# Weighted values as float32 products with two heads side by side, in a fused attention and SoLU kernel on one core

## The chip, the core and the metric

The kernel runs on one NeuronCore of a Trainium2 chip. Its engines each have their own instruction queue and run it in order: TensorE (PE in the profile, with its weight loads listed apart as PEld), VectorE (DVE), ScalarE (ACT), GpSimd (POOL) and SyncE (SP), which here only issues DMAs. The metric is the device time of one execution in microseconds; lower is better.

## What is computed

Attention with 4 sink keys and a causal window of 128 keys, and then a SoLU feed-forward layer on its output. Everything is float32.

```python
batch, n_heads, seq, head_dim = (4, 8, 768, 64);  n_sink, window = (4, 128)
scores = scale * np.matmul(q, k.transpose(0, 1, 3, 2))
keep = is_sink | in_window                    # rel = query - key, 0 <= rel < window
scores = np.where(keep, scores, -1000000000.0)
a = softmax(scores)
attn_out = np.matmul(a, v)
x = attn_out.transpose(0, 2, 1, 3).reshape(B * S, H * D)      # 3072 tokens, 512 wide
h = x @ w_in                                  # 512 -> 1024
sm = softmax(h); solu = h * sm
ln = (solu - mu) / np.sqrt(var + 1e-06) * g_ln
out = ln @ w_out                              # 1024 -> 512
```

q, k and v have the shape (4, 8, 768, 64). The weights arrive as 64-bit floats and are turned into 32-bit ones by integer work on the chip.

## The kernel before, in words

The 3072 tokens are worked in 24 chunks of 128. A chunk n is one block of 128 positions of one batch; `place(n)` (L472) gives its batch and its position c from 0 to 5, and two batches alternate, so that the chunk before in the same batch is n - 2. For c > 0 a chunk sees the keys of its own block, of the block before and of the sinks; for c = 0 (chunks 0, 1, 12 and 13) its own block alone.

TensorE multiplies in a rounded format (fp32r) at full rate, or in float32, which takes more passes. To keep float32 accuracy in fp32r most operands are split in a rounded first part and a rest, and two or three products are added. Chunks 0 and 1 are "native" (`native`, L551): they use plain float32 products for scores and values instead.

A chunk goes through these steps:

- `load_q`, `load_k`, `load_v`: DMAs on SP's queue. `turn_q`, `turn_k` (L533) transpose on TensorE; `take_*` (ACT) and `rest_*` (DVE) make the two parts; `swap_q` exchanges the halves by DMA.
- `score` (L604): two fp32r matmuls a head; `pick` and `mask` (DVE) choose the columns, add the mask and find the maximum; `exps` (ACT), `invert` (DVE), `normalise` (POOL).
- `turn_p` (L658) transposes the probabilities, four heads at a time; `p_hi` (ACT, L664) and `p_lo` (DVE, L668) split them; `part_new` and `part_old` (POOL, L675 and L682) cut out the part that belongs to the chunk's own block and that of the block before.
- `v_hi` (ACT, L502) and `v_lo` (POOL, L507) split v. `sink_values` (L513), once a batch, splits the first keys' values and spreads them over the pairs of heads; `sinks_hi`, `sinks_lo`, `turn_sinks`, `take_sinks` (L708, two ACT operations) do it for the sinks' probabilities.
- `value` (L715), one step for each of the four pairs of heads: for c > 0 five fp32r matmuls 256 wide into an accumulator of its own, in which first and second parts lie side by side. `gather` (DVE, L738) adds them, `shift` (L747) moves the halves that are on the wrong partitions by two DMAs, `tokens` (POOL, L755) adds these, and `x_hi` (ACT, L764) and `x_lo` (POOL, L768) split the result, half a chunk at a time. In the native chunks `value` writes two heads to the two halves of the partitions (L724), and there is no gather, shift or tokens.
- `hidden` (L775): eight steps of three fp32r matmuls, 512 wide. `highest`, `peak` (DVE), `solu_exp` (ACT), `solu` (DVE), `centre`, `square` (ACT), `variance` (DVE), `root` (POOL) make the SoLU and the normalisation. `turn_u`, `u_hi`, `u_lo`, then `project` (L846): eight steps of three fp32r matmuls; `scale` (ACT) and `store` (DMA).

The weights come in 16 blocks of 128 x 512: blocks 0 to 7 are w_in, 8 to 15 w_out. Each goes through `fetch_w` (DMA), `lower_w` (ACT, L419), `move_w`, `sign_w`, `rest_w` (DVE), `w_hi` (ACT, L453: the rounded part, for w_out times the gain). The second part is made with TensorE: `sum_w` (L446) multiplies the block in float32 by a negative diagonal from `gains` (L439), `less_w` (L463) adds the rounded part, and `w_lo` (ACT, L467) takes the negative of it:

```python
nc.tensor.matmul(t, st["dg", KT2 if j < NW1 else j - NW1], st["w", j], start=True, stop=False)
nc.tensor.matmul(st["ws", j], ident_r, part(wh, kt, cols), start=False, stop=True)
nc.scalar.mul(part(wl, kt, cols), st["ws", j], -1.0)
```

`idle` (L268) issues 33 float32 matmuls of the identity with itself, whose result nobody reads.

The order in which instructions enter the queues is written out by hand: every step has a time in `PLAN`, `FIRST`, `OWN` or `PLAN_W`, and the steps are issued in the order of these times (L876 to L881). The times only order the steps; the waits between engines are by semaphores. PSUM holds two buffers of one bank each for accumulators (`ps_acc`: values, sinks' transposes, project), two for scores and q and k transposes, two for the transposes of p and u, and two banks for h.

## Time and profile before

| | |
|---|---|
| three timed runs | 495.76, 496.22, 497.36 us (median 496.22) |
| the profiled execution | span 495.5 us from its first to its last instruction; its own time is not given apart from that |
| TensorE busy | 474.3 us (96%) |
| VectorE busy | 390.5 us (79%) |
| ScalarE busy | 354.2 us (71%) |
| GpSimd busy | 317.5 us (64%) |
| moved by DMA | 51.80 MB, mean 105 GB/s |
| granted TensorE clock, mean | 0.990 |

Matmuls are pipelined: the profile gives each one's start and a modelled end, so neighbours overlap. What one costs on TensorE's queue is the step from its start to the next one's. A float32 matmul that is not a transpose is two records. A group's row reads: line, engine, operation, output and inputs by the program's names, partitions x elements, count; then the busy time in us and the mean ns of one; then the idle time of the engine just before it and what ended most of it.

### The profile page before, as it was taken

Reading aid. Unit: us, or ns where it says so; the run is one execution under the profiler, and the core shown is the slowest. Engines: PE = TensorE matmul, PEld = TensorE weight load, DVE = VectorE, ACT = ScalarE, POOL = GpSimd, SP = SyncE. Lnnn points to the kernel's source line nnn. Section 1 sums busy time; section 2 is a strip of 40 time slices with the busy share of each in tenths; the row PEclk is TensorE's granted clock in tenths of the full one; section 3 lists DMA queues with packets and bytes.
Section 4 is the critical chain, followed back from the end, with each engine's and each line's share of the span. In section 5 each row is a group of like instructions: output and inputs, shape, how many; then the busy total and the mean of one; then the engine's idle time right before and its main releaser. Section 6 shows DMA issues by size and latency. Waiting matters only on the chain.

```text
span 495.5 us, 9225 instructions
## 1 busy us (share of the span) xinstructions
PE 474.3 (96%) x2697; PEld 395.1 (80%) x2697; DVE 390.5 (79%) x1195; ACT 354.2 (71%) x957; POOL 317.5 (64%) x439
## 2 busy tenths in 40 slices
PE   5988999999899999999999999999999999999994
PEld 5455767888788888888888888888888888888873
DVE  2888999899987588797799988888889879765631
ACT  3799997778776567776876787677777787675352
POOL 3677477587766557678646487576776776667610
PEclk9799999999999999999999999999999999999998
DMA  8976254354256363423365263364264262201101
GB/s 281 302 198 170 65 108 111 71 140 95 60 133 124 69 128 79 115 67 80 94 147 115 59 145 76 101 140 105 54 142 105 59 141 58 59 27 44 43 23 48
DMA packets 101100, 51.80 MB, mean 105 GB/s; under 512 B 78956, under 2 KB 90228, under 8 KB 101044
## 3 DMA queue, kind: packets, MB, share of 16 engines
q1 hardware_dynamic: 101044, 51.14, 42.6%
q8 instruction: 24, 0.39, 0.4%
q14 instruction: 32, 0.26, 0.2%
HBM read 27.53 MB, written 6.42 MB: 69 GB/s over the span
## 4 chain that ended last, share of the span: by engine, by line
PE 69%; DVE 15%; ACT 7%; issue 4%; POOL 3%; DMA 1%; SPq 0%; DVEq 0%; POOLq 0%
PE o L851 21%; PE h L782 20%; PE s L616 4%; PE utp L836 3%; PE av L731 3%; PE s L617 3%; PE av L734 3%; PE ptp L662 3%; DVE y L744 2%; DVE ring L589 2%; PE qt L536 2%; PE ws L451 2%; DVE sc L634 2%; PE kt L536 2%; PE av L736 2%
## 5 line engine op out<-in xcount | busy, mean ns | idle before, releaser
L851 PE MATMUL o<-w2h,uh 128*128 128x512 f32 x192 | 79.2, 413 | 0.0
L782 PE MATMUL h<-w1h,xh 128*128 128x512 f32 x192 | 77.5, 404 | 0.6 <-DVE u L804 0.6
L644 ACT ACTIVATE sc<-sc,nmx 128x136 f32<-128x136 f32 (+1 forms) x192 | 76.4, 402 | 1.7 <-DVE nmx L634 1.3
L782 PE MATMUL h<-w1l,xh 128*128 128x512 f32 x192 | 75.8, 395 | 0.0
L851 PE MATMUL o<-w2h,ul 128*128 128x512 f32 x192 | 75.7, 394 | 0.0
L782 PE MATMUL h<-w1h,xl 128*128 128x512 f32 x192 | 75.7, 394 | 0.0
L851 PE MATMUL o<-w2l,uh 128*128 128x512 f32 x192 | 75.7, 394 | 0.0
L744 DVE TENSOR_REDUCE y<-av 128x256 f32<-128x512 f32 x88 | 60.3, 686 | 19.5 <-PE av L736 18.8
L679 POOL TENSOR_SCALAR_AFFINE_SELECT pc<-pt 128x1024 fp32r<-128x1024 f32 x40 | 43.9, 1097 | 33.0 <-DVE pt L672 16.8
L655 POOL TENSOR_TENSOR sc<-sc,rs 128x544 f32<-128x544 f32 (+1 forms) x48 | 52.6, 1097 | 15.0 <-DVE rs L650 7.7
L634 DVE CUSTOM_DVE_ANT_0 sc<-s,bias 128x136 f32<-128x136 f32 (+1 forms) x192 | 54.3, 295 | 8.4 <-PE s L614 2.1
L616 PE MATMUL s<-ring,qT 128*128 128x264 f32 (+1 forms) x176 | 56.2, 321 | 2.8 <-DVE nmx L634 1.8
L771 POOL TENSOR_TENSOR xl<-xt,xh 128x256 fp32r<-128x256 f32 x44 | 32.5, 740 | 28.6 <-ACT xh L766 22.3
L617 PE MATMUL s<-ring,qX 128*128 128x264 f32 (+1 forms) x176 | 49.6, 284 | 0.3 <-DMA qX<-qT 0.3
L731 PE MATMUL av<-pc,vs 128*128 128x256 f32 x160 | 44.2, 299 | 1.3 <-ACT ob L856 0.9
L685 POOL TENSOR_SCALAR_AFFINE_SELECT pt<-pt 128x1024 fp32r<-128x1024 f32 x40 | 43.8, 1094 | 1.6
L782 PEld LDWEIGHTS h<-w1h,xl 128*128 128x128 f32 x192 | 36.1, 188 | 8.9 <-POOL xl L771 0.2
L840 ACT CAST uh<-utp 128x512 fp32r<-128x512 f32 x48 | 28.0, 586 | 21.2 <-PE utp L836 20.9
L844 DVE TENSOR_TENSOR ul<-utp,uh 128x512 fp32r<-128x512 f32 x48 | 33.0, 687 | 12.9 <-ACT uh L840 12.2
L851 PEld LDWEIGHTS o<-w2h,ul 128*128 128x128 f32 x192 | 36.1, 188 | 8.7 <-DVE ul L844 0.2
L616 PEld LDWEIGHTS s<-ring,qT 128*128 128x128 f32 x176 | 33.2, 188 | 12.0 <-issue 3.5
L584 ACT CAST ring<-kt 64x512 fp32r<-64x512 f32 x44 | 25.4, 578 | 22.9 <-DVE ring L589 21.8
(149 smaller groups left out, 1315.5 us busy)
## 6 DMA issues: line engine op xcount, KB each, us to landing
qX<-qT SPq DMA_DIRECT2D x88, 128.0 KB, 2.3
kn<-in_k_dram SPq DMA_DIRECT2D x24, 256.0 KB, 3.7
qn<-in_q_dram SPq DMA_DIRECT2D x24, 256.0 KB, 4.0
vn<-in_v_dram SPq DMA_DIRECT2D x24, 256.0 KB, 4.3
out_dram<-ob SPq DMA_DIRECT2D x24, 256.0 KB, 3.2
ysh<-y SPq DMA_DIRECT2D x88, 64.0 KB, 2.0
wraw<-in_moe_w_out_dram SPq DMA_DIRECT2D x8, 512.0 KB, 3.8
wraw<-in_moe_w_in_dram SPq DMA_DIRECT2D x8, 512.0 KB, 6.5
```

Of the source, the lines that this page charges most:

```text
L616: nc.tensor.matmul(o, st["qT", n, x][:, r, :], rhs, start=True, stop=False)
L617: nc.tensor.matmul(o, st["qX", n, x][:, r, :], rhs, start=False, stop=True)
L634: nc.vector.tensor_tensor_reduce(out=st["sc", n, hb][:, j, c0:c1], in0=st["s", n, h].rearrange("p a x -> p (a x)")[:, c0:c1], in1=bias0 if ...
L644: nc.scalar.activation(sc[:, i, c0:c1], sc[:, i, c0:c1], AF.Exp, bias=nmx[:, i:i + 1], scale=-1.0, accum_out=ssum[:, i:i + 1])
L655: nc.gpsimd.tensor_tensor(sc[:, :, c0:c1], sc[:, :, c0:c1], rs.unsqueeze(2).to_broadcast([P, HB, c1 - c0]), op=ALU.mult)
L679: nc.gpsimd.affine_select(pc, pt.bitcast(F32), pattern=[[0, HB * 2], [1, P]], compare_op=ALU.is_ge, fill=0.0, base=0, channel_multiplier=-1)
L685: nc.gpsimd.affine_select(pt, pt.bitcast(F32), pattern=[[0, HB * 2], [-1, P]], compare_op=ALU.is_ge, fill=0.0, base=-1, channel_multiplier=1)
L731: nc.tensor.matmul(acc[:, x], lhs, pc[:, 2 * jp + x], start=(x == 0), stop=(alone and x == 1))
L744: nc.vector.tensor_reduce(st["y", n, hb][:, jp], st["acc", n, pr].rearrange("p x s q -> p x q s"), axis=AX.X, op=ALU.add)
L782: nc.tensor.matmul(st["h", n][:, cols], a[:, kt % 2, :], w[:, kt, cols], start=(kt == 0 and m == 0), stop=(kt == KT1 - 1 and m == 2))
L844: nc.vector.tensor_tensor(ul, st["utp", n, g4], st["uh", n, g4].bitcast(F32), op=ALU.subtract)
L851: nc.tensor.matmul(st["o", n], a[:, kt % 4, :], part(w, kt), start=(kt == 0 and m == 0), stop=(kt == KT2 - 1 and m == 2))
```

## The change

- `value` becomes one step a chunk: for every pair of heads it multiplies plain float32 v by plain float32 probabilities, one head into the lower and one into the upper half of the partitions, for the chunk's own block and (c > 0) the block before, all into one accumulator of 512 columns. The native chunks use the same step.
- The sinks come first: `value_sinks` adds two fp32r matmuls, 512 wide. Their weights are a block-diagonal tile of the sink values (`sink_values`), and `take_sinks` spreads the probabilities over the four pairs by one DVE product.
- `v_hi`, `v_lo`, `p_lo`, `gather`, `shift` and `tokens` are gone, `p_hi` is called `take_p`, and the two selects work on half as many elements. `x_hi` (ACT) and `x_lo` (now DVE) read the accumulator once a chunk.
- The second part of a w_out block is one DVE operation (block times gain, less the rounded part) in place of `sum_w`, `less_w` and the ACT operation. w_in's blocks stay as they were. `idle` is gone.
- v has five buffers in place of two, p four of half the size in place of three.
- All the plans are replaced by one list, `ORDER`, with every step's place. In it w_in's block 6 is the first block to be fetched, lowered and moved; in the plan before, `fetch_w` began with block 10, `move_w` with block 6. 2614 steps stand in place of 3103.

```diff
-    def idle(_, j):
-        if "idle" not in st:
-            st["idle"] = ps_acc.tile([P, P], F32, tag="acc", name="idle")
-        nc.tensor.matmul(st["idle"], ident, ident, start=True, stop=True)
...
-    def gains(_, kt):
-        dg = st["dg", kt] = sb.tile([P, P], F32, tag="xt", name=f"dg_{kt}", bufs=2)
...
+    def gains(_, j):
+        st["minus"] = sb.tile([P, P], F32, tag="xl", name="minus", bufs=2)
+        nc.scalar.mul(st["minus"], ident, -1.0)
...
     def w_lo(_, j):
-        _, wl, _, kt, cols = blocks[j]
-        nc.scalar.mul(part(wl, kt, cols), st["ws", j], -1.0)
+        wh, wl, _, kt, cols = blocks[j]
+        if j < NW1:
+            nc.scalar.mul(part(wl, kt, cols), st["ws", j], -1.0)
+        else:
+            nc.vector.scalar_tensor_tensor(part(wl, kt, cols), st["w", j], g_sb[:, kt:kt + 1],
+                                           part(wh, kt, cols).bitcast(F32), op0=ALU.mult, op1=ALU.subtract)
...
+            vk = st["vsink", b] = sb.tile([P, 2, P], F32R, tag="vsink", name=f"vsink_{b}", bufs=2)
+            for x, m in enumerate((even, odd)):
+                cols = slice(x * D, (x + 1) * D)
+                nc.scalar.activation(vk[:, 0, cols], raw, AF.Copy, scale=m)
+                nc.vector.scalar_tensor_tensor(vk[:, 1, cols], raw, m, vk[:, 0, cols].bitcast(F32),
+                                               op0=ALU.mult, op1=ALU.subtract)
...
+    def take_p(n, hb):
+        pt = st["pt", n, hb] = sb.tile([P, HB, P], F32, tag="pt", name=f"pt_{n}_{hb}", bufs=4)
+        nc.scalar.copy(pt, st["ptp", n, hb])
...
-            for i, m in enumerate((even, odd)):
-                nc.scalar.activation(skt[:, i, :], tr.bitcast(F32), AF.Copy, scale=m)
+            skt = st["skt", n] = sb.tile([P, NPAIR, P], F32R, tag="skt", name=f"skt_{n}", bufs=2)
+            nc.vector.tensor_tensor(skt, st["skp", n].bitcast(F32).unsqueeze(1).to_broadcast([P, NPAIR, P]),
+                                    mine.to_broadcast([P, NPAIR, P]), op=ALU.mult)
+    def accumulator(n):
+        if ("acc", n) not in st:
+            st["acc", n] = ps_acc.tile([P, NPAIR, P], F32, tag="acc", name=f"av_{n}")
+        return st["acc", n]
+    def value_sinks(n, _):
         b, c = place(n)
+        if c > 0:
+            for t in range(2):
+                nc.tensor.matmul(accumulator(n), st["vsink", b][:, t, :], st["skt", n], start=(t == 0), stop=False)
+    def value(n, _):
+        alone = place(n)[1] == 0
+        acc = accumulator(n)
+        for r in range(NPAIR):
+            hb, jp = divmod(r, HB // 2)
+            terms = [(n, st["pt" if alone else "pc", n, hb])] + ([] if alone else [(n - 2, st["pt", n, hb])])
+            for i, (m, p) in enumerate(terms):
+                for x in range(2):
+                    nc.tensor.matmul(acc[ROWS[x], r, :], st["vn", m][:, 2 * r + x, :], p[:, 2 * jp + x, :],
+                                     start=alone, stop=alone or (r, i) == (NPAIR - 1, 1))
+    def x_hi(n, _):
+        xh = st["xh", n] = sb.tile([P, NPAIR, P], F32R, tag="xh", name=f"xh_{n}", bufs=2)
+        nc.scalar.copy(xh, st["acc", n])
+    def x_lo(n, _):
+        xl = st["xl", n] = sb.tile([P, NPAIR, P], F32R, tag="xl", name=f"xl_{n}", bufs=2)
+        nc.vector.tensor_tensor(xl, st["acc", n], st["xh", n].bitcast(F32), op=ALU.subtract)
...
-    for at, _, n, i, f in sorted(steps, key=lambda s: s[:4]):
+    for at in ORDER:
+        f, n, i = steps[at]
         f(n, i)
```

More of the change, by code (lines that the diff above doesn't have):

```diff
@@ L495, in load_v @@
     def load_v(n, _):
[L496 removed]
+        load(n, "vn", v, 5)
         b, c = place(n)
@@ new lines, in _banded @@
+    start = {
+        fetch_small: 3, round_ident: 1, gains: 1, scalars: 1, spread: 2, take_small: 2, masks: 3, outside: 1,
+        fetch_w: len(blocks), lower_w: len(blocks), move_w: len(blocks), sign_w: len(blocks), rest_w: len(blocks),
+        sum_w: NW1, w_hi: len(blocks), less_w: NW1, w_lo: len(blocks),
+    }
+    steps = [(f, 0, j) for f, k in start.items() for j in range(k) if k < NW1]
+    steps += [(f, 0, j) for j in range(len(blocks)) for f, k in start.items() if k >= NW1 and j < k]
@@ L881, in _banded @@
+    steps += [(f, n, i) for n in range(NCH) for f, k in stages.items() for i in range(k)]
+    for at in ORDER:
+        f, n, i = steps[at]
         f(n, i)
```

225 lines of the change are left out of this document (17 added, 208 removed), and 185 rows, old and new, of tables (ORDER, OWN).

## The prediction

> **What bounds the kernel now.** I read the page first, then the busy time by stretches (rows: stretch, its length, then busy time and instructions of PE, PEld, DVE, ACT, POOL; then the granted TensorE clock, DMA share, GB/s), then the chain of waits at the end, and last TensorE's instructions one by one where the trace holds the operations that the change adds.
>
> ```profile
> span 495.5 us, 9225 instructions
> PE 474.3 (96%) x2697; PEld 395.1 (80%) x2697; DVE 390.5 (79%) x1195; ACT 354.2 (71%) x957; POOL 317.5 (64%) x439
> ```
>
> ```profile
> 0.00:12.00 12.00, 6.91 (x46) 6.82 (x46) 2.38 (x6) 4.24 (x8) 3.43 (x18) 0.99 0.84 281
> 12.00:25.00 13.00, 11.63 (x39) 6.22 (x39) 11.25 (x30) 9.98 (x25) 8.54 (x13) 0.75 1.02 301
> 25.00:70.00 45.00, 40.79 (x216) 27.10 (x215) 39.95 (x124) 43.16 (x113) 30.16 (x47) 1.00 0.58 141
> 70.00:475.00 405.00, 401.24 (x2339) 344.43 (x2338) 331.47 (x1025) 290.46 (x805) 274.31 (x361) 1.00 0.40 93
> 475.00:496.00 21.00, 13.74 (x65) 10.58 (x63) 5.48 (x14) 6.32 (x10) 1.10 (x2) 0.93 0.08 29
> ```
>
> ```profile
> 473.93 2.11 PE h L782 x9
> ...
> 484.98 4.16 issue
> 489.13 0.69 ACT ob L856
> ```
>
> There are three regimes. From 70 to 475 us PE is busy for 401.24 of 405 us: here only what is on PE's own queue counts, and 3.8 us of gaps are all that better cover could win. Up to 70 us no engine is alone: ACT works 43.16 of the 45 us after 25, PE 40.79, DVE 39.95; ACT is the fullest. The tail (last project matmul, scale, store) has the same steps before and after, and I leave it alone. The profiled span is 495.5 us; the three timed runs are 495.76, 496.22 and 497.36, so I make the sum on the span and add 0.7 for the median. About 0.3% (1.5 us) is what a measurement here can tell from no change.
>
> **The change part by part: w_out's second parts leave PE.** Columns of the timeline: start, time, engine and line; what PE pays is the step from one start to the next, since the ends overlap.
>
> ```profile
> 72.47 1.02 PE L451 MATMUL ws<-wbits,dg 128*128 128x512 f32 x2
> 72.92 0.68 PE L731 MATMUL av<-pc,vs 128*128 128x256 f32 x1
> 73.44 0.28 PE L734 MATMUL av<-pt,vs 128*128 128x256 f32 x1
> 73.56 0.28 PE L731 MATMUL av<-pc,vs 128*128 128x256 f32 x1
> 73.67 0.28 PE L734 MATMUL av<-pt,vs 128*128 128x256 f32 x1
> 73.80 0.28 PE L736 MATMUL av<-skt,vsink 128*128 128x256 f32 x1
> 73.92 0.39 PE L465 MATMUL ws<-w2h,ident_r 128*128 128x512 f32 x1
> 74.14 0.60 PE L536 MATMUL qt<-ident,qn 128*128 128x128 f32 x4
> ```
>
> The float32 sum starts at 72.47 and the matmul after the next starts at 73.44; with 0.12 for the one between, the sum holds PE for 0.85 us. The subtraction on L465 takes 0.22 (73.92 to 74.14). Eight blocks: 8 x 1.07 = 8.6 us off PE. PE's records of this tile behind 70 us (three a block, float32 being two):
>
> ```profile
> 70.00:100.00 30.00, 2.88 (x6) 1.04 (x6) 1.17 (x2) 1.00 0.37 87
> ```
>
> So two blocks fall behind 70 us and six, 6.4 us, into the start-up.
>
> **The weighted values.** Before, a chunk behind the first of its batch issues 4 pairs x 5 fp32r matmuls at 0.118 (the steps 73.44 to 73.92): 2.36 us. After, it issues 16 float32 products of 64 columns of weights (two heads beside each other, so 8 pairs) and two 512-wide sink products. The trace has such float32 products in the first two chunks, on L724:
>
> ```profile
> 60.56 0.28 PE L617 MATMUL s<-ring,qX 128*128 128x264 f32 x1
> 60.77 0.66 PE L724 MATMUL xp<-pt,vn 128*64 128x128 f32 x8
> 61.36 1.12 PE L451 MATMUL ws<-wbits,dg 128*128 128x512 f32 x2
> ...
> 63.09 0.44 PE L724 MATMUL xp<-pt,vn 128*64 128x128 f32 x4
> 63.46 0.39 PE L616 MATMUL s<-ring,qT 128*128 128x264 f32 x1
> 63.69 0.28 PE L617 MATMUL s<-ring,qX 128*128 128x264 f32 x1
> 63.80 0.39 PE L465 MATMUL ws<-w2h,ident_r 128*128 128x512 f32 x1
> ```
>
> Each float32 product is two records, so x4 is one pair of heads and x8 two. One pair lasts 0.37 (63.09 to 63.46), two pairs 0.59: a further pair costs 0.22, not twice that, so the two heads do run at the same time. A burst also pays once: 0.37 - 0.22 = 0.15, then 0.09 before it (60.56 + 0.12 to 60.77) and 0.11 behind it (the step 63.46 to 63.69 is 0.23 where 63.69 to 63.80 is 0.12): 0.34 us. The change issues all of a chunk in one burst: 8 x 0.218 + 0.34 = 2.08, and the two sink products at 0.234 (nine in 2.11) are 0.47. So 2.55 against 2.36: +0.19 on 20 chunks, +3.8 us. The two later first-of-batch chunks: 4 x 0.218 + 0.34 = 1.21 against 8 x 0.118 = 0.94, together +0.5. The first two chunks go from four bursts of 0.56 to one of 1.21: -1.0 each, -2.0 in all, in the start-up. PE's queue in sum: -8.6 + 3.8 + 0.5 - 2.0 = **-6.3 us**.
>
> **What moves on the other engines.** Columns: line, operation, shape, count; busy time, mean ns; idle before it.
>
> ```profile
> L744 DVE TENSOR_REDUCE y<-av 128x256 f32<-128x512 f32 x88 | 60.3, 686 | 19.5 <-PE av L736 18.8 <-POOL pc L679 0.4 <-issue 0.2
> L434 DVE SCALAR_TENSOR_TENSOR wbits<-wraw,wbits 128x512 int32<-128x512 int32 x16 | 10.6, 689 | 0.0
> L844 DVE TENSOR_TENSOR ul<-utp,uh 128x512 fp32r<-128x512 f32 x48 | 33.0, 687 | 12.9 <-ACT uh L840 12.2
> L840 ACT CAST uh<-utp 128x512 fp32r<-128x512 f32 x48 | 28.0, 586 | 21.2 <-PE utp L836 20.9
> L761 POOL TENSOR_TENSOR xt<-y,ysh 64x256 f32<-64x256 f32 x44 | 32.2, 732 | 9.2 <-DMA ysh<-y 5.2 <-DVE z L812 3.3 <-DVE ul L844 0.7
> ```
>
> After 70 us everything gets lighter: DVE loses 60.3 us of gathers and the second halves of p and gets one 0.69 product for the sinks and one 0.69 subtraction (shape of L844) a chunk; ACT loses the casts of v; POOL loses the adds of L761 and L762, and SP's queue the 88 shifts. None of it is on the path, for PE is: price nothing, worth at most the 3.8 us of gaps. New waits there: value stands in PE's queue as one block behind take_p, the two selects and the sinks, with project and hidden queued behind it; and hidden waits for x_hi and x_lo (0.59 + 0.69, L840 and L844). Pricing the new order's PE steps as above, 1.0 to 1.1 us of other PE work lies between value and hidden in chunks 1, 21 and 23, over 2 us elsewhere: three waits below 1 us. I take the gaps as unchanged, between -3.8 and +4.
>
> The start-up is where cover can fail. The same columns for ACT between 25 and 70 us:
>
> ```profile
> L469 ACT ACTIVATE w2l<-ws 128x512 fp32r<-128x512 f32 x6 | 3.6, 597 | 0.2 <-PE ws L465 0.2
> L504 ACT CAST vs<-vn 128x256 fp32r<-128x256 f32 x6 | 2.3, 403 | 0.0
> ```
>
> ACT loses both, 6.0 us. DVE gains six products by then, 6 x 0.69 = 4.1 us (two sources in SBUF, shape of L434), and I set nothing off for the shorter sink values. DVE was busy 2.38 + 11.25 + 39.95 = 53.6 of 70 us and idle 16.4; to reach the same point it now works 57.7. Its first idle stretch:
>
> ```profile
> 4.23 0.66 ACT L421 ACTIVATE wbits<-wraw 128x512 f32<-128x512 f32 x1 [2.15 <-DMA wraw<-in_moe_w_out_dram]
> 8.92 0.66 ACT L421 ACTIVATE wbits<-wraw 128x512 f32<-128x512 f32 x1 [4.03 <-DMA wraw<-in_moe_w_in_dram]
> ...
> 9.62 0.76 DVE L425 TENSOR_SCALAR wbits<-wbits 128x512 int32<-128x512 int32 x2 [8.69 <-ACT wbits L421]
> ```
>
> A block has landed by 4.23, yet DVE's queue begins with the block lowered at 8.92. The new order fetches, lowers and moves block 6 first, so DVE can start at about 4.9, 4.7 earlier. DVE's path to that point: 57.7 + 16.4 - 4.7 = 69.4. PE's path: 70 less six sums (6.4) and the shorter first two chunks (2.0) = 61.6. The start-up ends between these. DVE's other 7.7 us of idle time (16.4 less 8.7) fell mostly while ACT was full, and ACT gets 6 us lighter; I take seven tenths of it, 5.4, as gone: 64.0, so **+2.4** against PE's path. The 22 records of idle matmuls behind 12 us, and the clock:
>
> ```profile
> 12.00:25.00 13.00, 0.49 (x2) 0.30 (x2) 0.75 1.02 301
> 25.00:70.00 45.00, 3.09 (x20) 2.54 (x20) 1.00 0.58 141
> ```
>
> ```profile
> 13.04 2.05 PE L451 MATMUL ws<-wbits,dg 128*128 128x512 f32 x2 [4.71 <-DVE wbits L434]
> ...
> 15.31 1.05 PE L536 MATMUL qt<-ident,qn 128*128 128x128 f32 x4
> ```
>
> They fill waits, between 0 and -3.6 us; I take 0. The 44 in front of 12 us (one unbroken run, until the wait of 4.71) did not keep the clock: the first sum takes 2.05 us against 1.02 later, the transposes 1.05 against 0.60. So taking them out should cost nothing. [...]
>
> Sum: 495.5 - 6.3 + 2.4 = 491.6, median **492.3**.
>
> **The rivals.** *Start-up shorter by ACT's relief.* If ACT alone set the start-up (43.16 of 45 us), it shortens by its 6.0 beside PE's own saving: 495.5 - 6.3 - 6 + 0.7 = 484. For it: ACT is fullest. Against it: DVE is close behind and gets fuller. *VectorE sets the start-up (slower).* DVE's 4.1 us land on a queue with 39.95 of 45 us used. If its idle time stays as it is, the start-up ends 4.1 later, PE's saving there is lost, and what remains is +4.3 of values and -2.1 of two late sums: 495.5 + 4.1 + 4.3 - 2.1 + 0.7 = 502.5. It turns to a loss once less than 6.3 of DVE's 16.4 idle us can be used (4.1 + 4.3 - 2.1). *Nothing measurable.* Had the whole of 12 to 25 us run at half clock, its 11.63 busy us at 0.75 would take 17.4, up to +4.4; that, or as many us of waits in the new order, gives 496. [...] *Accumulating products not side by side.* L724 starts a fresh sum each; the new ones add onto one bank. If pairs then took 0.44, 20 x 8 x 0.22 = +35: 527. Only the shared bank speaks for it, and L724's two heads share one too.
>
> **How the numbers follow.** Forecast (487 to 494.7) 0.52; ACT's relief (479 to 487) 0.18; nothing 0.11; VectorE sets the start-up (498 to 504) 0.14; not side by side 0.05. Faster 0.70, same 0.11, slower 0.19. The range from 481 to 501 leaves out the last case, half of the fourth and the end of the second, under 0.2. The forecast's own range is 487 to 494.7.
>
> **What would show it.** Right: 32 records of the value line in about 2.1 us, 0.22 a pair, a step of about 0.1 lost before and behind each burst; PE's gaps in the steady stretch still below 6 us; w_out's sums gone from PE; DVE above 90% before 65 us and ACT below. Wrong: pairs at 0.44, DVE's first work still at 9.6, hidden waiting for x_lo for over 1 us in most chunks, or a longer stretch at half clock.

## The result, and the profile after

The changed kernel takes **510.1 us** (median; runs from 507.5 to 511.4) against 496.7 us (495.8 to 497.4) for the kernel before: a ratio of 1.026, with a 95% interval of 1.023 to 1.029. It is slower by 13.4 us. I had forecast 492.3 us, with a range from 481 to 501.

The head of the page after shows less work on every engine, TensorE too, in a longer span:

```profile
span 505.7 us, 8964 instructions
PE 466.0 (92%) x2903; PEld 375.1 (74%) x2903; DVE 341.1 (67%) x1107; ACT 327.9 (65%) x837; POOL 153.3 (30%) x251
```

The busy time by stretches after, in the columns shown before (stretch, length, then PE, PEld, DVE, ACT, POOL, clock, DMA share, GB/s):

```profile
0.00:12.00 12.00, 2.19 (x8) 1.52 (x9) 5.77 (x11) 5.97 (x12) 6.39 (x20) 1.00 0.86 278
12.00:25.00 13.00, 9.78 (x39) 5.55 (x39) 12.20 (x35) 11.89 (x30) 11.66 (x22) 1.00 1.11 335
25.00:70.00 45.00, 35.63 (x209) 25.09 (x210) 39.60 (x122) 36.15 (x96) 19.01 (x26) 0.92 0.70 161
...
70.00:475.00 405.00, 394.12 (x2522) 323.99 (x2517) 276.47 (x926) 263.10 (x685) 113.33 (x180) 1.00 0.31 75
...
475.00:506.00 31.00, 24.24 (x135) 18.97 (x133) 7.06 (x16) 10.79 (x17) 2.90 (x5) 0.96 0.08 28
```

The clock's column reads 1.00 up to 25 us, but the trace's first record of the clock comes at 15.6 us, and the page counts what lies ahead of it as full. The same float32 sum takes 2.05 us ahead of that record and 1.12 behind it, so TensorE began at half clock:

```profile
11.83 2.05 PE L417 MATMUL ws<-wbits,minus 128*128 128x512 f32 x2
...
16.26 1.12 PE L417 MATMUL ws<-wbits,minus 128*128 128x512 f32 x2
```

In the long steady stretch PE is idle for 10.9 of 405 us (405 - 394.12), where it was for 3.8. In the start-up it is idle for 9.4 of 45 us, where it was for 4.2. The list of waits after names who ended TensorE's waits (us in total, times, longest; left out is a wait of 9.2 us for the first work of all):

```profile
...
PE h L694 <- DVE mx L701: 8.7, 8, 3.3
PE s L565 <- DVE ring L538: 4.6, 8, 1.1
PE s L563 <- ACT qf L507: 2.0, 1, 2.0
PE s L563 <- DVE nmx L583: 1.7, 4, 1.1
```

The row of `mx` did not exist before: a hidden step waits for `highest`, the maximum over h. Between 70 and 475 us lie 4.7 us of this row and 2.8 of the row of `ring`; before, `ring` had 0.4 there and `mx` nothing. The timeline after shows one of these waits (start, time, engine, line and tiles; in brackets the idle time before it and who ended it):

```profile
296.25 0.17 DVE L598 TENSOR_SCALAR rs<-ssum 128x4 f32<-128x4 f32 x1 [1.17 <-ACT sc L593]
296.46 0.18 DVE L599 RECIPROCAL rs<-rs 128x4 f32<-128x4 f32 x1
296.55 0.66 DVE L701 TENSOR_REDUCE mx<-h 128x1 f32<-128x512 f32 x1
...
297.27 0.49 PE L694 MATMUL h<-w1h,xh 128*128 128x512 f32 x1 [1.09 <-DVE mx L701]
```

The maximum of the first 512 columns of h ends at 297.21, and 0.06 us later TensorE begins with the other 512 columns. The maximum itself is late because VectorE's queue stood for 1.17 us in front of an inverse that waited for ScalarE. One late exponential has thus stopped TensorE by way of two steps that have nothing to do with it. The list of steps says why this can happen: in the order before, both maxima of a chunk stand behind all its hidden steps; in the new one the first maximum stands ahead of at least one hidden step of its own chunk in 16 of the 24 chunks.

**Where the 10.2 us of the two profiled runs lie.** I add up TensorE's queue with the prediction's own prices (hidden and project 3 x 0.2335 us a step, score 0.242, value 2.08 and so on), step by step in the order of each kernel, and take this sum from the step's start in the trace. What is left is the time lost by then, to waits and to half clock:

| | queue | lost by 90 us | lost behind 90 us | lost in all |
|---|---|---|---|---|
| before | 448.1 | 30.5 | 10.3 | 40.8 |
| after | 441.7 | 36.0 | 22.0 | 58.0 |
| difference | -6.4 | +5.5 | +11.7 | +17.2 |

With 0.6 us less in the tail behind the last matmul: -6.4 + 17.2 - 0.6 = 10.2, the difference of the spans, 505.7 and 495.5.

The medians differ by 13.4 us, so 3.2 us are not in this table. A run's time is 1.7 to 1.8 us more than its span. So the profiled run of the kernel before took about 497.3 us (an estimate), near the longest of its four, while that of the changed kernel (507.5) is the shortest of its four; the others took 509.9 to 511.4 us.

### The profile page after: what moved, and what is told of

It reads as the page before. It is cut to its first block, busy times and chain, and to the rows that moved or that the text cites. A ratio compares the mean times of both kernels' runs of the same rounds, so it can differ in the third digit from the quotient of the medians.

```text
span 505.7 us, 8964 instructions
## 1 busy us (share of the span) xinstructions
PE 466.0 (92%) x2903; PEld 375.1 (74%) x2903; DVE 341.1 (67%) x1107; ACT 327.9 (65%) x837; POOL 153.3 (30%) x251
## 4 chain that ended last, share of the span: by engine, by line
PE 68%; DVE 13%; ACT 9%; POOL 4%; issue 3%; DMA 2%; SPq 0%; ACTq 0%; DVEq 0%; POOLq 0%
PE h L694 22%; PE o L763 22%; PE av L674 5%; PE s L565 4%; PE s L566 4%; PE utp L748 3%; PE ptp L611 3%; DVE ring L538 3%; DVE mx L701 2%; DVE qT L516 2%; ACT sc L593 2%; PE qt L485 2%; ACT qT L510 1%; ACT ring L533 1%; PE av L664 1%
## 5 line engine op out<-in xcount | busy, mean ns | idle before, releaser
L694 PE MATMUL h<-w1h,xh 128*128 128x512 f32 x192 | 80.8, 421 | 9.9 <-DVE mx L701 8.7
L565 PE MATMUL s<-ring,qT 128*128 128x264 f32 (+1 forms) x176 | 54.0, 313 | 5.7 <-DVE ring L538 4.6
L620 POOL TENSOR_SCALAR_AFFINE_SELECT pc<-pt 128x512 f32<-128x512 f32 x40 | 25.5, 638 | 81.3 <-ACT pt L615 81.2
L694 PEld LDWEIGHTS h<-w1h,xh 128*128 128x128 f32 x192 | 36.1, 188 | 17.7 <-DVE mx L701 10.6
L694 PEld LDWEIGHTS h<-w1h,xl 128*128 128x128 f32 x192 | 36.1, 188 | 10.3 <-DVE xl L683 1.9
L763 PEld LDWEIGHTS o<-w2h,uh 128*128 128x128 f32 x192 | 36.1, 188 | 8.8 <-issue 2.4
L572 DVE COPY_PREDICATED s<-m_cur,s 128x128 f32<-128x128 int32 x96 | 27.4, 291 | 22.3 <-PE s L566 21.5
L615 ACT COPY pt<-ptp 128x512 f32<-128x512 f32 x48 | 27.7, 582 | 22.2 <-PE ptp L611 21.7
L701 DVE TENSOR_REDUCE mx<-h 128x1 f32<-128x512 f32 x48 | 32.5, 686 | 12.9 <-PE h L694 12.5
L538 DVE TENSOR_TENSOR ring<-kt,ring 64x512 fp32r<-64x512 f32 x44 | 30.3, 688 | 15.0 <-ACT ring L533 14.3
L763 PEld LDWEIGHTS o<-w2l,uh 128*128 128x128 f32 x192 | 36.2, 189 | 5.2
```

Of the source, the lines that this page charges most:

```text
L538: eng.tensor_tensor(t[ROWS[1 - x]], src[ROWS[x]], t[ROWS[x]].bitcast(F32), op=ALU.subtract)
L565: nc.tensor.matmul(o, st["qT", n, x][:, r, :], rhs, start=True, stop=False)
L572: nc.vector.copy_predicated(s[:, 0, 4:SEG], m_cur if c % 2 else m_prev, s[:, 1, 4:SEG])
L615: nc.scalar.copy(pt, st["ptp", n, hb])
L620: nc.gpsimd.affine_select(pc, st["pt", n, hb], pattern=[[0, HB], [1, P]], compare_op=ALU.is_ge, fill=0.0, base=0, channel_multiplier=-1)
L694: nc.tensor.matmul(st["h", n][:, cols], a[:, kt, :], w[:, kt, cols], start=(kt == 0 and m == 0), stop=(kt == KT1 - 1 and m == 2))
```

## The experiments

**The theories.** *Order*: the new arithmetic costs TensorE what I had worked out, and the loss comes from the new list of steps, whose waits I had not looked for. *Arithmetic*: float32 products and VectorE's new operations are what costs. *Idle matmuls*: taking them out cost the clock. Later two more were needed for the start-up: *VectorE* (its eight new products on a full queue) and *clock* (a thinner TensorE falls to half clock). In the diffs below a line of numbers is a line of `ORDER`.

**1. The old order for the new steps.**

```diff
 ORDER = (
-    68, 100, 0, 5, 6, 2, 59, 23, 143, 3, 93, 69, 70, 71, 72, 142, 4, 50, 101, 102, 103, 104, 86, 60, 245, 8, 10, 74,
+    100, 23, 0, 68, 59, 50, 93, 142, 143, 2, 86, 41, 101, 69, 60, 4, 3, 70, 102, 103, 61, 62, 63, 71, 5, 6, 8, 51,
...
```

> The changed kernel's steps, every operation as it is there, in an order taken from the plan of the kernel before (the new steps stand where the last of the steps that they replace stood; both maxima of a chunk behind all its hidden steps). Theory 1, the order lost the time: TensorE's queue is 6.4 us shorter than before and the waits fall back towards those of before, so the time lies between 487 and 497 us, well under the changed kernel's 510; in the trace the hidden steps no longer wait for the line of the maxima. Theory 2, the new arithmetic lost it (float32 products, VectorE's new products): the time stays above 505. Theory 3, the missing idle matmuls lost it through the clock: it stays within 3 us of 510, with a mean granted clock under 0.985.

Measured: 511.0 us, 1.032 (1.029 to 1.035) of the kernel before. By the time alone theory 1 had fallen. The trace splits it. The steady stretch from 100 to 475 us, in the kernel before, in the changed kernel and in this one:

```profile
100.00:475.00 375.00, 371.72 (x2168) 319.60 (x2167) 305.03 (x944) 267.81 (x736) 255.17 (x336) 1.00 0.40 93
```

```profile
100.00:475.00 375.00, 365.51 (x2344) 300.90 (x2344) 250.84 (x849) 242.36 (x629) 105.64 (x169) 1.00 0.30 73
```

```profile
100.00:475.00 375.00, 371.70 (x2425) 309.98 (x2424) 255.13 (x869) 244.40 (x653) 108.90 (x175) 1.00 0.34 80
```

TensorE's gaps are 3.3, 9.5 and 3.3 us. In the old order the new arithmetic waits no more than the old one did. But the start-up of this run has lost 49.0 us by 90 us, where the kernel before had lost 30.5 and the changed one 36.0. So the order is to blame behind 90 us, and something else, which the old order takes badly, sits in the start-up.

**2. Both maxima behind the hidden steps, nothing else.** 1551 and 1552 are hidden steps 2 and 3 of chunk 13, 1555 and 1556 steps 6 and 7, 1557 and 1558 the maxima:

```diff
-    1648, 1640, 1705, 1713, 1721, 1728, 1797, 1799, 1729, 1732, 1551, 1552, 1557, 1796, 1798, 1800, 1466, 1468, 1470,
...
+    1556, 1557, 1711, 1719, 1727, 1731, 1558, 1559, 1807, 1462, 1736, 1815, 1823, 1471, 1560, 1709, 1717, 1725, 1730,
```

> The changed kernel with one thing altered in its order: the two steps that take the maximum of h come behind the last hidden step of their chunk, wherever the order had put the first one between hidden steps. Theory 1: the eight waits of hidden steps for the maximum go (8.7 us by the page's row), a little comes back as a later softmax, and the time is 5 to 8 us under the changed kernel's, 502 to 505. Theories 2 and 3: no more than 1.5 us changes, 508.5 to 511.

Measured: 505.1 us (501.7 to 507.3), 5.0 under the changed kernel (1.018 of the kernel before, 1.012 to 1.023). The row of hidden steps waiting for the maxima is gone, and the steady stretch has 6.7 us of gaps in place of 9.5:

```profile
100.00:475.00 375.00, 368.32 (x2367) 303.17 (x2367) 251.10 (x854) 243.90 (x631) 106.38 (x171) 1.00 0.30 73
```

As theory 1 expected, at the lower end: of 8.7 us some come back in waits elsewhere. The 5.0 us are not all gaps of the steady stretch. From 100 us on the gaps shrink by 2.8. Between 25 and 70 us, where the longest of the eight waits stood (3.3 us), TensorE is idle for 6.8 us in place of 9.4, and between 70 and 100 us for 4.1 in place of 1.4.

**3. The mirror: an early maximum in the kernel before.** If the order alone makes this wait, it can be put into the old kernel.

```diff
+    line = [(n, i, f) for _, _, n, i, f in sorted(steps, key=lambda s: s[:4])]
+    for n in range(NCH):
+        ends = [max(line.index((n, KT1 * x + kt, hidden)) for kt in range(KT1)) for x in range(NH)]
+        x = ends.index(min(ends))
+        line.insert(ends[x] + 1, (n, x, highest))
...
```

> The kernel before, all its arithmetic as it is, with one step a chunk moved: the maximum over that half of h which is complete first is taken right behind that half's last hidden step, so in front of the other half's last one (the old plan takes both maxima behind all hidden steps). Theory order (TensorE must wait for VectorE's maximum before it writes on to h, although it writes other columns): about 0.7 to 1.0 us in each of 24 chunks, 505 to 520 us, and a row of hidden steps waiting for the maxima that the kernel before does not have. If those waits belong to the new arithmetic: 495 to 498.

Measured: 521.7 us, 1.051 (1.050 to 1.053): one moved step a chunk costs 25 us. The waits and the steady stretch of this kernel:

```profile
PE h L782 <- DVE mx L789: 19.7, 23, 1.3
```

```profile
100.00:475.00 375.00, 355.91 (x2070) 302.37 (x2069) 300.89 (x935) 259.09 (x721) 243.01 (x320) 1.00 0.40 91
```

The row has 0.86 us a time, in 23 chunks, though the step that waits writes other columns than the maximum reads. That wait belongs to the order and to no arithmetic.

**4. w_out's second parts alone, in the kernel before.** The next five runs take the start-up apart. First the products on VectorE with TensorE's sums gone:

```diff
-        nc.scalar.mul(part(wl, kt, cols), st["ws", j], -1.0)
+        if j < NW1:
+            nc.scalar.mul(part(wl, kt, cols), st["ws", j], -1.0)
+        else:
+            nc.vector.scalar_tensor_tensor(part(wl, kt, cols), st["w", j], g_sb[:, kt:kt + 1],
+                                           part(wh, kt, cols).bitcast(F32), op0=ALU.mult, op1=ALU.subtract)
...
     def sum_w(_, j):
+        if j >= NW1:
+            return
```

> The kernel before with one part of the change alone: w_out's second parts as one VectorE product each, with their sums, subtractions and ScalarE operations gone, in the old order and with the idle matmuls kept. TensorE loses 8 x 1.07 = 8.6 us of its queue, six of the eight before 70 us; VectorE gains 8 x 0.69 us. Theory 1 (VectorE sets the start-up, the rest is order): the start-up gains nothing or loses up to 4 us, the two late sums give 2.1, so 494 to 499 us. My prediction's own step (+2.4 against TensorE's path with 6.4 saved): 490 to 493.

Measured: 508.0 us, 1.024 (1.017 to 1.030): 8.6 us less on TensorE's queue, and 12.0 us slower. Every theory missed. Two things change at once here, VectorE's queue and TensorE's, so the next two runs take one each. **Dead sums**: VectorE makes the products and TensorE still makes the sums, which nobody reads. **No sums**: TensorE's sums are gone and VectorE gets nothing. Each has a smaller change beside it: dead sums leaves out ScalarE's eight operations, no sums GpSimd's diagonals.

```diff
 # dead sums: w_lo as above, sum_w and less_w as in the kernel before
...
 # no sums: sum_w and less_w return as above, and w_lo for w_out is
+            nc.scalar.mul(part(wl, kt, cols), part(wh, kt, cols).bitcast(F32), 0.0001)
```

> The kernel before with w_out's second parts made by one VectorE product each, while TensorE still issues their sums and subtractions as before, into a bank that nobody reads; ScalarE's operations are gone. Theory clock (TensorE made too thin in the start-up falls to half clock, as in the run with that part alone: 27 us of half clock in its trace against 6.8 before): TensorE stays as full as before, one stretch of half clock, 494 to 499 us. Theory VectorE (the eight products of 0.69 us on a full VectorE cost the time): 502 to 508, as with that part alone.

> The kernel before without w_out's sums and subtractions on TensorE and without VectorE's products: ScalarE makes a stand-in from the rounded part (the rounded part times 0.0001), so the computation of w_out's second parts is left out. Theory clock: TensorE is thin although VectorE has no more work than before, several stretches of half clock, 499 to 506 us. Theory VectorE: the 8.6 us taken off TensorE are won, 487 to 492.

Measured: dead sums 502.5 us, 1.013 (1.011 to 1.015); no sums 500.6 us, 1.007 (1.005 to 1.010). The two changes cost 6.2 and 4.3 us, and together 12.0: they nearly add up, and neither wins anything. The first is what theory VectorE expected, the second what theory clock did. Waits of TensorE between 25 and 70 us in the kernel before, and then with dead sums:

```profile
PE s L614 <- DVE nmx L634: 1.0, 2, 0.6
PE s L616 <- DVE nmx L634: 0.7, 3, 0.3
...
PE kt L536 <- DVE nmx L634: 0.6, 1, 0.6
```

```profile
PE kt L540 <- DVE nmx L638: 2.0, 1, 2.0
PE s L620 <- DVE nmx L638: 1.2, 3, 0.6
...
PE s L618 <- DVE nmx L638: 1.0, 2, 0.5
```

Six products of 0.69 us stand in VectorE's queue ahead of the masks (nmx), and TensorE waits for the masks: 4.2 us in these rows, 2.3 before. The masks are the part with a name. All gaps of TensorE from 25 to 70 us grow from 4.2 to 7.2 us, and from 70 to 100 us from 0.5 to 2.3. VectorE's products ahead of the masks are my second rival, in the old order, at 6.2 us where I had put 4.1. With the sums gone, TensorE has waits where the sums stood, and its clock answers. The stretches that the run with that part alone (experiment 4's first) spent at half clock, then those of the run without sums:

```profile
11.82:18.64 6.82, 5.95 (x14) 3.19 (x14) 6.79 (x12) 3.84 (x8) 6.24 (x9) 0.50 1.04 312
22.06:28.88 6.82, 5.81 (x15) 3.30 (x16) 6.50 (x18) 4.04 (x14) 2.37 (x2) 0.50 0.78 251
35.71:45.95 10.24, 8.68 (x30) 5.48 (x29) 9.05 (x18) 6.64 (x14) 4.74 (x9) 0.50 0.24 54
73.26:76.67 3.41, 3.09 (x8) 2.30 (x9) 2.80 (x13) 2.44 (x4) 2.27 (x3) 0.50 0.19 31
```

```profile
13.12:30.18 17.06, 15.42 (x43) 8.82 (x43) 14.45 (x35) 11.89 (x29) 9.98 (x15) 0.50 0.93 297
37.01:40.42 3.41, 3.15 (x12) 2.50 (x12) 3.38 (x7) 2.95 (x6) 2.38 (x4) 0.50 0.09 21
67.73:74.56 6.83, 6.55 (x24) 4.87 (x21) 5.04 (x18) 5.98 (x15) 4.46 (x5) 0.50 0.72 131
```

Both spend 27.3 us at half clock; the kernel before spends 6.8:

```profile
11.65:18.48 6.83, 5.44 (x14) 3.25 (x14) 6.80 (x12) 3.86 (x8) 5.02 (x7) 0.50 0.97 285
```

At most half of TensorE's busy time there is lost: 23.5 / 2 = 11.8 us against 5.4 / 2 = 2.7 before.

**5. Idle matmuls where the sums stood.** This tells the clock from the waits. The diff is against the run without sums.

```diff
         if j >= NW1:
-            return
+            t = st["ws", j] = ps_tr.tile([P, NB], F32, tag="tr", name=f"ws_{j}")
+            for i in range(4):
+                nc.tensor.matmul(t[:, i * P:(i + 1) * P], ident, ident, start=True, stop=True)
+            return
...
+            nc.tensor.matmul(st["ws", j][:, 0:P], ident, ident, start=True, stop=True)
```

> As the run without w_out's sums and without VectorE's products (ScalarE's stand-in, so w_out's second parts are not computed), but where a sum and a subtraction stood on TensorE, five idle matmuls of the identity with itself stand (five times 128 columns in float32, about the same time), which wait for no other engine. Theory clock: TensorE stays full, one stretch of half clock in the start-up, 494 to 498 us, faster than without the idle matmuls (500.6) although TensorE has 8 us more to do. Theory waits between engines: 500 us or more.

Measured: 498.0 us, 1.002 (0.999 to 1.004), 2.6 us faster than without these matmuls, as theory clock expected, and one stretch of half clock:

```profile
13.84:17.26 3.42, 3.31 (x12) 2.18 (x11) 3.42 (x7) 0.84 (x3) 3.07 (x5) 0.50 0.90 267
```

So in the old order TensorE's sums were free and worth having: useless work in their place brings back 2.6 of the 4.3 us.

**6. Only the two late blocks.** I had counted two sums behind 70 us as sure.

```diff
     def sum_w(_, j):
+        if j in (12, 14):
+            return
```

> The kernel before with VectorE's product in place of sum, subtraction and ScalarE's operation for two of w_out's eight blocks alone, 12 and 14, whose sums TensorE does behind 70 us, where it is full and VectorE is not. My prediction's own step for these two (2 x 1.07 us off TensorE's queue, VectorE's products covered): 494 to 495 us. If VectorE or the clock take it back there as they do in the start-up: 496 to 498.

Measured: 498.3 us, 1.0034 (1.0022 to 1.0047). Slower, by 1.7 us. The busy time from 78 to 90 us before, and here:

```profile
78.00:90.00 12.00, 11.52 (x63) 9.30 (x62) 10.06 (x35) 8.78 (x24) 10.02 (x14) 1.00 0.53 123
```

```profile
78.00:90.00 12.00, 9.78 (x49) 7.99 (x48) 10.70 (x33) 7.28 (x19) 9.66 (x14) 0.86 0.51 116
...
82.08:85.50 3.42, 3.42 (x14) 3.02 (x14) 3.42 (x15) 2.70 (x7) 3.35 (x5) 0.50 0.28 64
```

TensorE, 2.1 us early, waits for the probabilities of chunk 3 and for the exchanged parts of the queries of chunk 4 (0.8 and 1.2 us in the list of waits), and falls to half clock for 3.4 us. In the whole of this run there is no more half clock than before, 6.8 us, since the stretch of the start-up is 3.4 us shorter; so the trace shows where the 2.1 us went, and not what makes the run 1.7 us longer. Its full row before did not mean that it set the end there: the sums filled what would have been waits.

**7. The same part, undone in the changed kernel.** Once with the sums back on TensorE at the place of VectorE's products, once with VectorE's products replaced by ScalarE's stand-in.

```diff
+            t = ps_acc.tile([P, NB], F32, tag="acc", name=f"ws_{j}")
+            nc.tensor.matmul(t, st["dg", j], st["w", j], start=True, stop=False)
+            nc.tensor.matmul(t, ident_r, part(wh, kt, cols), start=False, stop=True)
+            nc.scalar.mul(part(wl, kt, cols), t, -1.0)
...
 # the other: in place of VectorE's product
+            nc.scalar.mul(part(wl, kt, cols), part(wh, kt, cols).bitcast(F32), 0.0001)
```

> The changed kernel with w_out's second parts as before: sum and subtraction on TensorE (in a bank of the accumulators, at the place of VectorE's product in the order), ScalarE's negative, the diagonals from GpSimd; VectorE's eight products are gone. TensorE has 8.6 us more in its queue. If that part loses time in the new order too, as in the old one (+11.7 us alone): 500 to 507. If it wins there what I predicted of it: 513 to 518. In between: start-up waits cover the sums.

> The changed kernel with VectorE's eight products for w_out's second parts replaced by a stand-in on ScalarE (the rounded part times 0.0001), so that their computation is left out: VectorE has 5.5 us less to do, six eighths of it in the start-up, ScalarE about 5 us more. Theory VectorE sets the changed kernel's start-up: 505 to 507 us. Theory waits between engines and the clock set it: within 2 us of the changed kernel's 510.

Measured: 521.7 us (1.051, 1.049 to 1.052) with the sums back, above every case expected, and 507.7 us (1.027, 1.020 to 1.035) with the stand-in, between the two theories. In the new order the sums would cost 11.6 us, more than their 8.6, and VectorE's products at most a few (-2.4, an interval that holds zero). The part that costs 12.0 us in the old order wins 11.6 in the new one, as far as a sum put at the product's place tells it.

**8. Idle matmuls in the changed kernel.**

```diff
+    idle(22)
+    waits = {("score", 0, 1): 5, ("score", 0, 0): 2, ("turn_q", 1, 0): 2, ("turn_p", 0, 1): 2, ("sum_w", 0, 3): 2}
...
+        extra = waits.get((f.__name__, n, i))
+        if extra:
+            idle(extra)
```

> The changed kernel with idle matmuls put back: 22 at the front and 13 in five of its waits of the start-up. Theory 3 (their absence cost the time through the clock): the mean granted clock is at least 0.99 and the time 4 us or more under the changed kernel's. Theory 1: the clock may rise from 0.98 to 0.99, the time moves by 0 to -2.5 us, since VectorE sets the start-up.

Measured: 513.3 us (1.034, 1.032 to 1.037), 3.2 slower than without them. Both theories missed on the wrong side; that the missing idle matmuls cost the time has fallen. What a full clock would be worth this run can't tell, for it did not have one: its trace has 17.1 us of half clock, and its runs granted clocks of 0.980 to 0.988.

**9. A better order for the same instructions.** First two pieces: the changed kernel's list up to 56 us of TensorE work, the old plan behind it.

```diff
-    137, 32, 45, 107, 248, 144, 56, 80, 159, 175, 250, 262, 267, 350, 138, 865, 155, 15, 16, 283, 351, 1070, 190, 192,
+    137, 32, 45, 107, 248, 144, 56, 80, 159, 175, 250, 262, 267, 350, 138, 155, 15, 16, 283, 351, 190, 192, 183, 31,
...
```

> The changed kernel, every operation as it is there, in an order of two pieces: the changed kernel's own up to 56 us of TensorE work (about 92 us of time; both maxima behind the hidden steps), and the plan of the kernel before, with the new steps in place of the old, from there on. Theory order (the new arithmetic costs nothing in the steady stretch, the waits there come from the new order; the old order loses only in the start-up): TensorE's queue of 441.7 us, 35 us lost by the cut, 10 behind it: 486 to 491 us, faster than both kernels. If the steady waits belong to the new arithmetic: 500 or more.

Measured: 504.0 us (1.016, 1.011 to 1.020). A miss by 13 us, most of it at the joint. There a score waits 3.5 us, until 96.31, for exchanged parts of its queries; from 93.6 us on, during this wait, TensorE is at half clock for 10.2 us, and the time lost grows from 34.9 us at 90 us to 47.4 at 150. From 150 to 480 it grows by 5.9 more; in the changed kernel by 19.1.

Then the steps behind the joint were shifted by a few places each (568 of 2614 by more than five), and twice more, each time against the waits that the last trace showed; in the second and third round the steps from about 45 us on too. The diff shows a line of the order in two pieces and what stands there after the first round.

```diff
-    240, 241, 242, 243, 244, 576, 584, 592, 597, 515, 332, 578, 151, 254, 200, 199, 172, 167, 152, 303, 196, 148,
+    240, 241, 242, 243, 244, 576, 584, 592, 597, 515, 332, 578, 151, 254, 762, 333, 601, 200, 199, 172, 167, 152,
...
```

> The changed kernel, every operation as it is there. Its order is that of the order in two pieces (the run before, 504 us), its first 480 steps untouched; behind them steps were shifted by some places to take away the waits of TensorE that the traces show, above all the 4.0 us and 1.5 us at the joint (turn_p of chunk 4), behind which its trace has 10 us of half clock. Theory order: at the joint and later nothing of the new arithmetic has to wait; TensorE's queue of 441.7 us, 35 us lost by 92 us, 5 to 11 behind it: 484 to 491 us. If the waits come back elsewhere, because leads that the traces show too coarsely are too short: 495 to 500. If the new arithmetic itself must wait: 502 or more.

> The changed kernel, every operation as it is there, in the searched order with steps from the 230th on (about 45 us) shifted once more, to take away the waits that its trace shows at 56, 95, 188 and 372 us. Theory order: five to eight us less than the searched order, 490 to 495 us, faster than both kernels by a little. If the start-up is held by VectorE's and ScalarE's work and not by the order: 497 to 500.

> The changed kernel, every operation as it is there, in the order shifted once more (494.1 us), of which steps from the 200th on (about 43 us) were shifted a third time, to take away the waits that its trace shows at 58 (2.5 us), 94 to 107 and 259 to 332 us. Theory order: 2 to 4 us less, 490 to 492. If what is left in the start-up is VectorE's and ScalarE's work and the half clock between 24.6 and 38.2 us, before the steps that were shifted: 493 to 495.

Measured: 499.7 us (1.006, 1.003 to 1.009), 494.1 us (0.997, 0.995 to 1.000) and **492.5 us (0.991, 0.987 to 0.994)**. The last is faster than both kernels, with every operation of the changed one. The first missed theory order's number and lies where waits that come back elsewhere were expected; the time lost by 100 us was 38.7 us where I had reckoned with 35 at the joint. The third gave 1.6 us, a little less than the 2 to 4 expected, and lies between what its two theories said. Its steady stretch and what TensorE still waits for between 70 and 475 us:

```profile
100.00:475.00 375.00, 373.74 (x2429) 313.43 (x2429) 252.22 (x856) 244.22 (x634) 106.04 (x172) 1.00 0.33 78
```

```profile
PE s L566 <- DVE ring L539: 0.5, 2, 0.3
PE s L567 <- DMA qX<-qT: 0.4, 1, 0.4
PE h L695 <- DVE u L717: 0.3, 1, 0.3
```

Gaps of 1.3 us in 375, less than the 3.3 of the kernel before. By the sum used above it has lost 35.3 us by 90 us and 6.1 behind, with a stretch of 13.7 us at half clock in the start-up (24.4 to 38.0 us), twice that of the kernel before.

**10. Idle matmuls in the waits of these orders.**

```diff
 # in the first of these orders
+    waits = {('score', 1, 0): 9, ('score', 1, 5): 5, ('turn_q', 2, 0): 6, ('turn_p', 0, 1): 6, ('score', 2, 1): 6, ('turn_p', 2, 0): 9, ('value', 3, 0): 9}
...
 # in the second: the first five
```

> The changed kernel in the searched order (499.7 us, runs between 495.4 and 502.6 with granted clocks of 0.972 to 0.988) with 50 idle matmuls, put into seven waits that its trace shows (0.97 to 2.3 us each, before score, turn_q, turn_p and value up to 95 us), each a little shorter than its wait. Theory clock (TensorE's dips there cost the half clock behind them, 25.6 to 32.5 and 56.4 to 59.8 us in its trace): the clock is 0.99 or more in every run and the time 494 to 496. Theory waits alone: 499 to 501, as without them; if the idle matmuls get in the way of real work, more.

> As the order shifted once more, with 32 idle matmuls put into five waits between 22 and 41 us. Theory clock: the half clock between 25 and 33 us goes, 1 to 3 us less than without them, and the runs lie closer together. Theory waits alone: no difference over 1 us, or slower.

Measured: 501.3 us (1.008, 1.005 to 1.011) against 499.7 without them, and 497.2 us (1.001, 0.998 to 1.005) against 494.1. No time was won; theory clock missed both. The granted clock reads higher, 0.991 and more in nine runs of the first and 0.995 against 0.979 in the profiled runs of the second, but it counts what lies ahead of the trace's first record as full clock. In the second that record comes at 27.0 us, without the idle matmuls at 14.3. The same float32 sum, without and with the idle matmuls:

```profile
16.10 1.12 PE L418 MATMUL ws<-wbits,minus 128*128 128x512 f32 x2
```

```profile
16.84 2.07 PE L418 MATMUL ws<-wbits,minus 128*128 128x512 f32 x2
```

So this run began with 12.7 us more of half clock, in steps that are the same in both programs: the first idle matmul starts at 27.12, and the scores ahead of it are already 4.4 us late (26.45 against 22.10). Behind the fifth row the values of chunk 0 are 1.9 us late (40.65 against 38.78). There the idle matmuls held up nothing that the trace shows; why the median is 3.1 us longer stays open. In the profiled run of the first (505.7 us, the longest of its ten) they did: two rows of 12 records ran at half clock, 2.93 and 2.67 us long where they take 1.60 and 1.50 at full clock, and the scores, 2.8 us late ahead of the first row, were 7.2 us late behind the fourth. That explains this long run and not the median.

## Why the prediction was wrong

**Right: TensorE's queue, -6.3 us.** The values came out as priced. The timeline after, one chunk: two sink products, eight pairs, the next matmul:

```profile
320.07 0.71 PE L664 MATMUL av<-skt,vsink 128*128 128x512 f32 x2
320.71 0.44 PE L674 MATMUL av<-pc,vn 128*64 128x128 f32 x4
320.98 0.39 PE L674 MATMUL av<-pt,vn 128*64 128x128 f32 x4
321.20 0.39 PE L674 MATMUL av<-pc,vn 128*64 128x128 f32 x4
...
322.29 0.39 PE L674 MATMUL av<-pt,vn 128*64 128x128 f32 x4
322.61 0.50 PE L763 MATMUL o<-w2h,uh 128*128 128x512 f32 x1
```

A pair every 0.22 us, accumulating, as in the fresh sums before, and 2.54 us for all (320.07 to 322.61) where I had 2.55. In the other chunks whose sinks and values stand together it is 2.45 to 2.54 us too, once 3.17. The rival that accumulating products are not side by side is out.

**Wrong: "I take the gaps as unchanged, between -3.8 and +4".** This is the step that failed. Behind 90 us the change lost 11.7 us more than the kernel before. I looked for new waits only where the arithmetic was new (value, and hidden behind x_hi and x_lo), and found three small ones. The waits came from steps whose arithmetic had not changed: `highest` between hidden steps (experiments 2 and 3) and scores that stand just behind the keys they need (the row of `ring`), 4.7 and 2.8 us between 70 and 475 us. The diff had the list; "everything gets lighter" and "price nothing" are statements on load, and these are waits of order, which a lighter engine does not take away. Experiment 1 and the last order, with gaps of 3.3 and 1.3 us from 100 to 475 us, show that the new arithmetic needs none of them.

**Mis-sized: the start-up, +2.4.** It came to +5.5 by 90 us. The pieces were near: VectorE's busy time to 70 us is 5.77 + 12.20 + 39.60 = 57.6, where I had 57.7, and its queue does begin earlier, though at 6.08 and not at 4.9:

```profile
6.08 0.45 DVE L397 TENSOR_SCALAR wbits<-wbits 128x512 int32<-128x512 int32 x1 [5.15 <-ACT wbits L393]
```

What failed is the frame, TensorE's path less its removed sums as a floor that the start-up could come down to. Experiments 4 to 6 show that in the old order the sums were not on the path at all, and that without them TensorE waits and falls to half clock: "So two blocks fall behind 70 us" and are saved there is wrong by 2.1 + 1.7 us. The forecast for the new order was less wrong than that; that its start-up was laid out without the sums would explain it, as far as experiment 7 tells.

**The clock, taken as 0.** For the idle matmuls this stands: put back, they bring nothing (experiments 8 and 10). For the clock itself it does not. One of my signs of being wrong was "a longer stretch at half clock", and it came: by the durations TensorE's work from 10.7 to 15.6 us and by the clock that from 25.8 to 32.7 ran at half speed, 11.8 us in place of 6.8. At most half of TensorE's busy time there is lost, 9.1 / 2 = 4.6 us against 2.7 before, so the clock can be up to 1.9 of the 5.5 us of the start-up. Half clock came with a thinner TensorE elsewhere too: experiments 4 and 5 have 27.3 us of it without the sums and 3.4 with idle matmuls in their place, which were 2.6 us faster. A busy TensorE did not always end it soon: in the run with w_out's part alone the stretch at half clock from 35.71 to 45.95 us lasted 10.24 us, with TensorE busy for 8.68 of them.

**The rivals.** "VectorE sets the start-up" at 502.5 came nearest; "not side by side" at 527, the other one on the slow side, fell by the price of a pair. The mechanism of the first holds in the old order (6.2 us) and explains at most a few us of the change itself (the stand-in of experiment 7: -2.4, not apart from zero). The result of 510 us lies outside all the cases that I had listed: only *Nothing measurable* named waits in the new order, at up to 4.4 us, and none looked for them in the list of steps.

**Open.** Of the 5.5 us lost in the start-up I can name the half clock (up to 1.9), one wait of 3.3 us for a maximum and waits for qf, ring and masks, but no single cause, and these do not add up without overlap. Behind 90 us, 2.8 us of gaps are shown to be the maxima's; that the rest is order is shown by the orders that lose less, not row by row.

## What to carry to other kernels

The same instructions took from 492.5 to 511.0 us in seven orders, more than any operation of this change was worth: when a change comes with a new order, go through the list for each buffer that one engine reads while another still writes to it, with unchanged steps included. A full engine may be full of work that was laid into its waits, so take such work away on paper only after asking what it would wait for in its place. And where parts can be set apart, do all four combinations: here two parts cost 6.2 and 4.3 us, and both together 12.0.

## What the runs showed of the hardware

Between the first record of the clock and 470 us, half clock came in stretches of 3.41 and 17.06 us (the run without sums), 6.83 (the kernel before), 10.24 (w_out's part alone) and 13.7 (the last order), all multiples of 3.41 us. A window is here a piece of this length, counted from where a stretch of half clock begins. In the first shifted order a window with 1.46 of 3.41 us busy, whose longest wait is 2.1 us, was followed by one at half clock:

```profile
52.96:56.37 3.41, 1.46 (x9) 1.00 (x7) 3.23 (x5) 3.14 (x10) 2.11 (x5) 1.00 0.51 118
56.37:59.78 3.41, 3.24 (x20) 3.00 (x22) 2.40 (x12) 3.10 (x9) 1.09 (x1) 0.50 1.11 231
```

In the changed kernel a wait of 3.3 us, from 51.6 to 54.9, was followed by none. On the grid that the trace's stretches of half clock give, it lies across two windows:

```profile
49.74:53.15 3.41, 1.83 (x14) 1.32 (x12) 2.97 (x8) 1.34 (x5) 2.28 (x2) 1.00 0.17 38
53.15:56.56 3.41, 1.64 (x7) 1.37 (x8) 2.06 (x3) 2.32 (x7) 2.12 (x6) 1.00 0.50 114
56.56:59.98 3.42, 2.69 (x18) 2.17 (x17) 1.90 (x4) 2.67 (x11) 0.14 (x1) 1.00 1.06 221
```

So the length of a wait alone did not decide it; the busy share of a window did, nearly. I cut all 19 traces, from the first record of the clock to 470 us, into windows on each one's own grid. Of the windows at full clock, 28 had TensorE busy for less than 47.5%, and every one was followed by half clock; 2440 had it busy for more than 60%, and all but two were followed by full clock. The 18 between went either way, nine each.

The mean granted clock hid half clock at the start of one run: with a mean of 0.995 it ran its float32 sums of 512 columns in 2.07 and 1.92 us up to 25.3 us (experiment 10), where 1.12 and 1.02 are the time at full clock.
